# Attention and MLP in one fused kernel: one table for the order of all engines, banks and places

## The chip, the cores and the metric

The kernel runs on one core of a Trainium2 chip. The core has five engines, each with its own instruction stream that it works through in order: TensorE (PE in the profile) for matmuls, VectorE (DVE), ScalarE (ACT), GpSimd (POOL) and SyncE (SP). Here SP does nothing but issue DMA transfers. ScalarE and GpSimd can issue DMAs too. Engines wait for each other with semaphores. PSUM, into which TensorE writes, is used as a ring of 8 banks of 128 x 512 numbers. The metric is the device time of one execution in microseconds (us).

## The reference, cut to what matters

The shapes are: x 1 x 2048 x 448, wqkv 448 x 1344, wo 448 x 448, w1 448 x 1792, w2 1792 x 448, all in bfloat16; 16 heads of 28 columns.

```python
xn = layernorm(x)
q, k, v = split(xn @ wqkv)                    # 16 heads, Dh = 28
p = softmax(q @ k.T * Dh ** -0.5)             # 2048 x 2048 for each head
s = concat_heads(p @ v) @ wo
g = silu(gelu(xn @ w1 + b1) @ w2 + b2)
out = x + s * g
```

## The kernel before

**Tiling.** The 2048 rows of x are four chunks of 512 rows, the 16 heads are four groups of four. A block is one head group for one chunk of queries, so there are 16 blocks, head group outside, chunk inside. A block has 64 scores; a score is one 128 x 512 tile (128 keys, 512 queries, one head) in one PSUM bank, so the kernel has 1024 of them. ScalarE takes the exponential of 776 scores, two or three banks in one instruction. VectorE handles the other 248, in 62 groups of four, another way: it scales and shifts the score into a 16-bit integer whose bits are those of an approximate bfloat16 exponential. Two further copies of each such group, with a constant added to the bits, stand beside it, and p·v sums all three with differently scaled values. These are the 124 shifted copies. A copy is one VectorE instruction (`fs` with `tensor_scalar` on 128 x 2048 16-bit numbers) or two GpSimd halves (`tensor_tensor` on 128 x 512 32-bit numbers). For 5 groups the two shifted copies are first added to each other, so that p·v has two terms: twice by VectorE, three times by a GpSimd DMA that accumulates. A block's p·v is gathered in a PSUM bank and taken out (evacuated) by VectorE, in one or more parts.

**Last quarter of K.** D = 448 is three slices of 128 rows and one of 64. The 64-row slice of a projection can be done as two matmuls of 32 rows, which stand beside scores in TensorE's row mode, or as one full matmul ("joined" or not in the code; the first are called products in score phases here). A padded score takes q from `qpad` with the other heads' rows at zero and runs in the other mode. Before, 21 scores are of this kind. Seven groups of matmuls of the identity with zeros (`filler`) keep TensorE busy; they compute nothing that is used.

**Order.** `schedule` (L1141) lets generators (`p_score`, `p_expq`, `p_ln`, ...) run against a cost model and so records the operations in `K.ops`; each has an engine, a function, a semaphore count and what it needs. `arrange` (L441) takes each engine's operations in recorded order and reorders them by `ORD` (L15): each number says which of those left comes next. `ORD` has rows for PE, ACT, DVE and POOL and none for SP, so SP issues its DMAs as recorded. `place` (L469) puts uses of PSUM into banks, some by `BANKS` (L89). `emit_all` (L553) then writes the five streams, with a wait for each need not yet covered. Nearly every instruction goes through the small wrapper `_Eng`, which is why the profile shows L258 for all of them.

**Start.** `loads` (L1378) issues the first DMAs. In what follows R*n* is the operation recorded with number *n*. SP issues, in this order:

| loads on SP | what | KB |
|---|---|---|
| R16, R17 | x chunk 0, tiles 0 and 1 | 112 each |
| R21, R22 | first head group's columns of the q and k weights, K slices 2 and 3, into `stg` (named `h` in the profile) | 56, 28 |
| R24 | x chunk 1, tiles 1 to 3 | 336 |
| R25, R26 | v weights | 336, 56 |
| R27, R28 | x chunks 2 and 3 | 448 each |
| R29 to R32 | the other head groups' q and k weights | 3 x 168, 84 |
| R33, R34 | w1 | 1344, 224 |
| R249, R250 | x of chunks 0 and 1, copied from DRAM to the output in DRAM | 448 each |

ScalarE's queue issues R18 (x chunk 0, tiles 2 and 3, 224 KB), R19 and R20 (K slices 0 and 1 of the first head group's weights, 56 KB each) and R23 (x chunk 1, tile 0, 112 KB).

R19 to R22 count on one semaphore, `s_w["wqk"]`, and their reader waits until all four are in:

```python
        lw(0, 4 * DH, K.s_w["wqk"], K.b_stg, 6.1, (ACT, ACT, SP, SP))
```

Readers of `stg` are the ScalarE copies into `wq` and `wk` (128 x 224 twice, 128 x 448 once), after which TensorE can do the first q and k projections, and GpSimd's square of the weights (`h<-h`, 128 x 448), from which come the corrections for q. On ScalarE's stream every exponential stands behind these copies. On GpSimd's stream the selector `bsel`, the fill of `vaug` and the layer norm of part of chunk 1 stand behind the square.

**End.** The last chunk's output goes out in 8 stores of 112 KB, seven on SP and one on ScalarE's queue. Each waits for its own sum on VectorE.

Of the kernel before, what the change touches and what calls it, by code (L numbers as in the profile page):

```python
# [6 lines left out]
dt = mybir.dt  # L7
# [7 lines left out]
ORD = {  # L15
# [39 lines left out]
    ),  # L55
    'ACT': (
# [8 lines left out]
    ),  # L65
    'DVE': (
# [21 lines left out]
TO = ()  # L88
# [10 lines left out]
H = 16  # L99
# [198 lines left out]
class _Kernel:  # L298
# [58 lines left out]
    def add(self, t, need, name):  # L357
# [5 lines left out]
        o.no = name  # L363
        return o

    def to(self, ms, us, at, engines, n, ports):


        K = self
# [2663 lines left out]
```

## Time and profile before

| what | us |
|---|---|
| median of 3 runs (lowest, highest) | 410.63 (409.8, 410.68) |
| span of the profiled execution | 408.0 |
| TensorE busy | 395.1 |
| ScalarE busy | 398.1 |
| VectorE busy | 343.5 |
| GpSimd busy | 194.8 |

The span goes from the first to the last instruction; the time of a run is 2.6 us longer than it (410.63 - 408.0). In the views a row has the line, engine, operation, the program's names of output and input tiles, shapes, and "x" with a count; after the bar come busy us, the mean ns of one, and idle time before them with what ended it. Consecutive ScalarE instructions overlap in the records: the next starts before the last one's end is shown. So its pace is read from start to start. Rows of a timeline begin with the start and the length; rows with a count join instructions that follow each other. Rows of the DMA view have the KB of one transfer and the median time from its issue to its landing.

### The profile page before, as it was taken

To read this page: it belongs to the slowest core of one execution; us is meant where nothing else is said; L and a number is where in the kernel's file an instruction comes from. 1 tells how busy PE (TensorE), PEld (TensorE's weight loads), DVE (VectorE), ACT (ScalarE), POOL (GpSimd) and SP (SyncE) were. 2 spreads that over 40 slices of the span, in tenths; PEclk is the share of its full clock that TensorE was granted. 3 is DMA by queue.
4 is the path that set the end of the run, shared out by engine and by line. 5 is a ranking of instruction groups with operands and counts; after the bars stand their busy time and mean duration, and the time that the engine had idled before them with its cause. 6 is when DMAs were issued, how large, how long until landed. Compare 5 with 4: busy or idle time off the path is not lost.

```text
span 408.0 us, 14601 instructions
## 1 busy us (share of the span) xinstructions
PE 395.1 (97%) x6157; PEld 144.6 (35%) x6157; DVE 343.5 (84%) x596; ACT 398.1 (98%) x409; POOL 194.8 (48%) x221
## 2 busy tenths in 40 slices
PE   6899999999999999999999999999999999999996
PEld 5443233333332333332223444332333323333363
DVE  8967688896679889989898127999998999798976
ACT  5999999999999999999999999999999999999995
POOL 7595457649982563254652231156156013555041
PEclk9999999999999999999999999999999999999999
DMA  8902110000101010100331100220010003200065
GB/s 244 305 2 42 4 31 2 16 20 19 29 3 31 2 25 11 34 2 2 77 116 30 30 3 6 55 53 15 18 34 2 4 31 57 64 20 21 14 114 134
DMA packets 18783, 17.54 MB, mean 43 GB/s; under 512 B 8941, under 2 KB 15421, under 8 KB 18686
## 3 DMA queue, kind: packets, MB, share of 16 engines
q1 hardware_dynamic: 16734, 13.55, 12.0%
q0 software_dynamic: 1008, 2.49, 3.8%
q8 instruction: 48, 0.79, 0.9%
q10 hardware_dynamic: 976, 0.57, 0.5%
q14 instruction: 17, 0.14, 0.1%
HBM read 12.54 MB, written 2.88 MB: 38 GB/s over the span
## 4 chain that ended last, share of the span: by engine, by line
PE 59%; ACT 28%; issue 7%; DVE 4%; DMA 1%; POOL 0%; ACTq 0%; DVEq 0%; POOLq 0%
PE ring L258 59%; ACT P L258 16%; ACT h L258 8%; ACT xnT L258 3%; DVE st L258 1%; DVE h L258 1%; DVE xnT L258 1%; DMA x_sb<-in_A_x_dram 1%; DVE vaug L258 0%; DVE x_sb L258 0%; ACT w L258 0%; DVE qT L258 0%; POOL h L258 0%; DVE mv L258 0%; DVE w L258 0%
## 5 line engine op out<-in xcount | busy, mean ns | idle before, releaser
L258 ACT ACTIVATE P<-ring 128x1024 bf16<-128x1024 f32 (+1 forms) x236 | 253.8, 1246 | 1.0 <-PE ring L258 1.0
L258 PE MATMUL ring<-qT,kT 32*128 32x512 bf16 (+2 forms) x1131 | 131.7, 359 | 4.2 <-ACT P L258 1.0
L258 ACT ACTIVATE h<-ring 128x1024 bf16<-128x1024 f32 (+2 forms) x93 | 101.3, 1204 | 2.0 <-PE ring L258 2.0
L258 PEld LDWEIGHTS ring<-qT,kT 32*128 32x128 bf16 x1131 | 36.3, 91 | 121.8 <-ACT P L258 48.1
L258 DVE TENSOR_SCALAR vaug<-ring 128x512 uint16<-128x512 f32 x92 | 60.8, 683 | 5.5 <-PE ring L258 4.8
L258 PE MATMUL ring<-xnT,w 128*32 128x512 bf16 (+1 forms) x880 | 65.3, 381 | 0.0
L258 PE MATMUL ring<-w,h 128*32 128x448 bf16 x896 | 58.5, 356 | 0.0
L258 PE MATMUL ring<-P,vaug 128*32 128x512 bf16 (+2 forms) x606 | 57.9, 351 | 0.2
L258 POOL TENSOR_TENSOR qT<-x_sb,E_sb 128x512 bf16<-128x512 f32 x15 | 17.4, 1162 | 64.6 <-DMA x_sb<-recs 38.0
L258 ACT ACTIVATE xnT<-ring 128x1024 bf16<-128x1024 f32 (+2 forms) x41 | 47.6, 1199 | 0.5 <-PE ring L258 0.5
L258 POOL TENSOR_TENSOR rc<-rs,mone 128x16 f32<-128x16 bf16 x11 | 33.3, 3023 | 28.7 <-DMA rs<-E_sb 14.6
L258 DVE TENSOR_SCALAR w<-ring 128x512 uint16<-128x512 f32 x52 | 34.5, 683 | 2.0 <-PE ring L258 1.7
L258 PEld LDWEIGHTS ring<-xnT,w 128*32 128x32 bf16 (+1 forms) x880 | 21.7, 96 | 28.0 <-issue 6.6
L258 PEld LDWEIGHTS ring<-w,h 128*32 128x32 bf16 x896 | 19.3, 95 | 24.4 <-issue 14.8
L258 PE MATMUL ring<-h,vaug 128*32 128x512 bf16 x201 | 25.1, 383 | 0.0
L258 PE MATMUL ring<-xnT,wq 128*32 128x512 bf16 (+2 forms) x240 | 22.6, 379 | 0.2 <-DVE w L258 0.2
L258 PEld LDWEIGHTS ring<-P,vaug 128*32 128x32 bf16 x606 | 17.3, 95 | 13.6 <-issue 7.4
L258 PE MATMUL ring<-xnT,wk 128*32 128x512 bf16 (+2 forms) x244 | 21.8, 379 | 0.3 <-DVE xnT L258 0.2
L258 DVE TENSOR_SCALAR h<-ring 128x512 uint16<-128x512 f32 x28 | 18.9, 685 | 3.3 <-PE ring L258 3.0
L258 POOL TENSOR_TENSOR qsq<-qT 128x512 bf16<-128x512 bf16 x12 | 13.0, 1079 | 17.0 <-DVE x_sb L258 13.9
L258 DVE CAST qT<-ring 128x512 bf16<-128x512 f32 x15 | 10.3, 688 | 12.7 <-PE ring L258 12.7
L258 DVE CAST h<-ring 128x512 bf16<-128x512 f32 x24 | 16.5, 688 | 4.8 <-PE ring L258 4.8
(207 smaller groups left out, 616.8 us busy)
## 6 DMA issues: line engine op xcount, KB each, us to landing
x_sb<-recs SPq DMA_DIRECT2D x60, 64.0 KB, 2.1
w<-in_B_w_dram SPq DMA_DIRECT2D x1, 1568.0 KB, 7.3
w<-in_B_w_dram SPq DMA_DIRECT2D x1, 1344.0 KB, 8.7
x_sb<-in_A_x_dram SPq DMA_DIRECT2D x2, 448.0 KB, 6.6
out_dram<-in_A_x_dram SPq DMA_DIRECT2D x2, 448.0 KB, 10.6
out_dram<-h POOLq DMA_DIRECT2D x4, 224.0 KB, 4.6
out_dram<-h SPq DMA_DIRECT2D x7, 112.0 KB, 4.4
xnT<-wq POOLq DMA_DIRECT2D x1, 512.0 KB, 6.6
```

Source lines behind the costliest of these rows:

```text
L258: return lambda *a, **k: f(*[real(x) for x in a], **{n: real(x) for n, x in k.items()})
```

## The change

`ORD`, `TO` and `BANKS` go. One table, `PLAN`, takes their place. It is one list of some 3,000 tokens, and the streams of all five engines, SP included, are filled by walking along it. `R`*n* keeps the recorded operation *n* (with its banks behind a slash); the other letters build operations anew: `S` a score, `C` a padded score, `X` exponentials on ScalarE with the cells they are written to, `A` a VectorE score, `H` a shifted copy on VectorE, `G` one half of a shifted copy on GpSimd, `M` the addition of two shifted copies on VectorE, `V` a p·v product, `E` an evacuation of a block, `P`, `J` and `Q` a projection's full matmul, its 32-row halves, and its evacuation. The list begins:

```diff
-ORD = {
...
-TO = ()
-BANKS = {
...
+PLAN = """
+    R0 R16 R24 R2 R28 R5 R4 R6 R3 R18 R1 R35/6 R19 R20 R23 R36/6 R37/6 R250 R17 R29 R39/6 R262 R7 R38 R42 R8 R27 R21 R30 R294 R33 R31 R32 R9 R34 R10
+    R11 R25 R26 R22 R40/6 R41/6 R15 R46 R44/6 R45/6 R50 R48 R47/6 R43 R49/6 R53 R51/6 R52 R54/6 R81 R57/6 R60 R55 R58 R56 R59/6 R64 R61/6 R99 R68/6
...
```

The new `arrange` walks along the table and appends each operation to its engine's stream; for a kept operation it takes the needs over, for a new one it works them out from what last used the bank, the cell or the copy's place:

```diff
-            for d in ORD.get(name, ()):
-                at.append(left.pop(d))
...
+        plan = [(x[0], *([int(z) for z in y.split(",") if z] for y in x[1:].split("/"))) for x in PLAN.split()]
...
+        for x in plan:
...
+                ps = range(4) if t == "H" else range(4 // PH * a[2], 4 // PH * a[2] + 4 // PH)
...
+                o = new(DVE if t == "H" else POOL, fn, need, ("h", m0), True)
...
+            seq[o.E].append(o)
+        K.emit_all(seq)
```

`emit_all` now puts one wait per semaphore ahead of an instruction, that for the highest count, where before it put one for each need not yet covered.

The work changes in these counts:

| | before | after |
|---|---|---|
| exponential instructions of ScalarE: two banks, three, one | 286, 68, 0 | 275, 67, 25 |
| scores handled by VectorE | 248 | 248 |
| shifted copies by VectorE, by GpSimd | 92, 32 | 53, 71 |
| additions of two copies: VectorE, GpSimd DMA | 2, 3 | 6, 0 |
| projections whose last slice stands in score phases | 14 | 11 |
| padded scores | 21 | 12 |
| filler groups | 7 | 0 |
| evacuations of blocks by VectorE | 34 | 29 |

SP's first DMAs now come in this order (R294 is a load of b1 in 1792 pieces of two bytes, 3.5 KB, which before was issued 40 us into the run): R16, R24, R28, R250, R17, R29, R27, R21, R30, R294, R33, R31, R32, R34, R25, R26, R22. R249 comes near the end of the kernel. ScalarE's queue still issues R18, R19, R20, R23, now ahead of its table load. On GpSimd's stream the square of the weights (R81) is followed by R82, R12, R13, R83, R14 (`bsel`), R84, then the fills of `vaug` and the layer norm (R120, R132, R124, R136).

SP's last stores come in the order R3054, R3075, R3031, R3037, R3025, R3062, R3094, where before it was R3025, R3031, R3037, R3054, R3062, R3075, R3094. The VectorE sum ahead of R3075 (R3074) is third from last on VectorE. One multiplication of silu (R3071, 128 x 448 on ScalarE), which before came after the last exponential, now stands between the exponentials near the end.

More of the change, by code (lines that the diff above doesn't have):

```diff
@@ L98 @@
+"""
 D = 448
@@ L239, in get @@
     def get(self):
-        i = self.use.base + self.off if self.off is not None else slice(self.use.base, self.use.base + self.use.n)
+        p = self.use.pos
+        i = p[self.off] if self.off is not None else slice(p[0], p[-1] + 1, p[1] - p[0] if len(p) > 1 else 1)
         x = self.ring[:, i, :]
@@ L277 @@
 class _Op:
-    __slots__ = ("E", "fn", "sem", "by", "cnt", "need", "dur", "lat", "mode", "rows", "port", "start", "kind", "fixed", "spec", "banks", "use", "no", "turn")
+    __slots__ = ("E", "fn", "sem", "by", "cnt", "need", "dur", "lat", "mode", "rows", "port", "start", "kind", "fixed", "spec", "banks", "use", "no", "turn", "rd", "wr")
 class _Task:
@@ L336, in op @@
         o.sem, o.cnt = h if h else (None, 0)
+        if spec and spec[0] in ("exp", "a", "h", "evac", "last"):
+            for b in writes:
+                self.first_w.setdefault(id(b), ([b.w] if b.w is not None else []) + [x for x in b.r if x is not None])
         o.need = [("X", x) for x in self.pre[E]]
@@ L441, in arrange @@
-    def arrange(self):
-        seq = {}
-        for x in TO:
-            (self.to if len(x) > 2 else self.join)(*x)
-        self.chain_up()
-        for E, name in ((PE, "PE"), (ACT, "ACT"), (DVE, "DVE"), (POOL, "POOL"), (SP, "SP")):
-            lst = [o for o in self.ops if o.E == E]
-            at, left = [], list(range(len(lst)))
-            for d in ORD.get(name, ()):
-                at.append(left.pop(d))
-            seq[E] = [lst[i] for i in at + left]
-        self.place(seq)
-        self.emit_all(seq)
@@ L542, in chain_up @@
-    def chain_up(self):
-        chain = [o for o in self.ops if o.port and o.start is not None]
-        for at, o in sorted(self.put_port[::-1], key=lambda x: -x[0]):
-            chain.insert(at, o)
-        last = {}
-        for o in chain:
-            for E, kind in ((POOL if o.E == DVE else DVE, "P"), (o.E, "Q")):
-                if E in last:
-                    o.need.append((kind, (last[E].sem, last[E].cnt)))
-            last[o.E] = o
+        of = lambda h: K.by_h[(id(h[0]), h[1])]
@@ new lines, in arrange, with kind @@
+        K.number()
+        name = lambda o: o.fn.__qualname__.split(".<locals>.")[0].split(".")[-1] + ("" if o.fn.__qualname__.endswith("<lambda>") else "." + o.fn.__qualname__.split(".")[-1])
+        evac = {o.spec[1]: o for o in K.ops if o.spec and o.spec[0] == "ev" and not (o.spec[1][0] == "qk" and o.spec[1][2] == 0)}
+        keys = sorted(evac, key=str)
+        core = ("s", "sc", "exp", "a", "h", "evac", "last")
+        def kind(o):
+            s = o.spec
+            if name(o) == "filler.f" or o.kind == "x" or name(o) == "p_expq" and s is None:
+                return "gone"
+            if not s:
+                return "rest"
+            if s[0] == "pv":
+                return "rest" if s[2][0][0] // 64 == NBLK - 1 else "core"
+            if s[0] in core:
+                return "core"
+            if s[0] in ("pr", "ev") and s[1] in evac:
+                return s[0]
+            return "rest"
@@ new lines, in arrange @@
+        kd = {id(o): kind(o) for o in K.ops}
+        writer, unit_at, opens = {}, {}, {}
+        for o in K.ops:
+            if o.spec and o.spec[0] in ("s", "sc", "pv"):
+                for b, (_, h) in zip(o.rd, [x for x in o.need if x[0] == "R"]):
+                    if kd[id(of(h))] in ("rest", "ev"):
+                        writer.setdefault(id(b), {})[(id(h[0]), h[1])] = h
+            if o.spec and o.spec[0] == "h":
+                unit_at.setdefault(o.spec[1], {}).update({o.spec[5]: o.spec[2], o.spec[4]: 0})
@@ new lines, in arrange @@
+        final = {o.spec[1]: o for o in K.ops if o.spec and o.spec[0] == "last"}
+        plan = [(x[0], *([int(z) for z in y.split(",") if z] for y in x[1:].split("/"))) for x in PLAN.split()]
+        ops, seq = {o.no: o for o in K.ops}, {E: [] for E in (PE, ACT, DVE, POOL, SP)}
+        full = {x[1][0] for x in plan if x[0] == "P" and x[1][1] == KT - 1}
+        merged = {x[1][0] for x in plan if x[0] == "M"}
+        grouped = {x[1][0] // 4 * 4 for x in plan if x[0] == "A"}
+        left = [sum(1 for x in plan if x[0] == "V" and x[1][0] // 64 == b) for b in range(NBLK)]
@@ new lines, in through @@
+        def through(p):
+            c, s = kd[id(p)], p.spec
+            if c == "rest" or c == "ev":
+                return [p]
+            if c == "pr":
+                return [evac[s[1]]]
+            if c == "core" and s[0] == "last":
+                return [p]
+            if c == "core" and s[0] in ("s", "sc", "pv"):
+                b = (s[1] if s[0] != "pv" else s[2][0])[0] // 64
+                return [final[b]] if b in final else []
+            return []
+        was = {id(o): list(o.need) for o in K.ops}
@@ new lines, in arrange @@
+        K.ops = [o for o in K.ops if kd[id(o)] == "rest" or o in list(evac.values()) or o in list(final.values())]
+        bank = {i: [] for i in range(NRING)}
+        cell, lane = {}, {}
+        sc, ex, ap, sh, pads, acc, burst, begun, part = {}, {}, {}, {}, {}, {}, {}, {}, set()
+        pr, done, last_pad, port, e1 = {}, set(), [], None, None
+        pad_of = [o for o in K.ops if name(o) == "p_pad" and o.E == SP]
+        shc = [o for o in K.ops if name(o) == "p_pad.f"][0]
+        vs = {o.spec[1:]: o for o in K.ops if o.spec and o.spec[0] == "vs"}
@@ new lines, in new, with take, cells @@
+        def new(E, fn, need, spec, port=False):
+            K.n_new += 1
+            o = K.op(E, fn, (K.evsem[E], 10 ** 6 + K.n_new), 1, (), (), "t", 0.1, 0.05, "", (), port, spec=spec)
+            o.need += need
+            return o
+        def take(i):
+            need = [("A" if p.E != PE else "W", H(p)) for p in bank[i]]
+            bank[i] = []
+            return need
+        def cells(cs):
+            reg, k = K.pslots[cs[0]]
+            n = len(cs)
+            st = cs[1] - cs[0] if n > 1 else 1
+            return reg[:, k:k + st * (n - 1) + 1:st, :]
@@ new lines, in used, with room @@
+        def used(x):
+            return [("A", H(p)) for p in [p for p in x if not p.spec or p.spec[0] not in ("exp", "a")] or x]
+        def room(toks, at, key):
+            if key in at:
+                return used(at[key])
+            need, seen = [], set()
+            for b in toks:
+                for h in first.get(id(b), ()):
+                    for p in through(of(h)):
+                        if id(p) not in seen:
+                            seen.add(id(p))
+                            need.append(("A", H(p)))
+            return need
@@ new lines, in lanes, with begin @@
+        def lanes(u):
+            if 11 <= u <= 13:
+                return [NP + 42 - F0 + 4 * (u - 11) + k for k in range(4)]
+            if 14 <= u <= 15:
+                return [NP + 56 - F0 + 4 * (u - 14) + k for k in range(4)]
+            return []
+        def begin(u):
+            cs = lanes(u)
+            need = []
+            if cs:
+                for c in cs:
+                    need += room([K.b_P[c]], cell, c)
+            else:
+                need += room(K.b_U[u], lane, u)
+            for c in cs:
+                cell[c] = []
+            lane[u] = []
+            return need
@@ new lines, in touch, with score @@
+        def touch(u, o):
+            lane[u].append(o)
+            for c in lanes(u):
+                cell[c].append(o)
+        first = K.first_w
+        def score(m, b, pad):
+            b0, j, pc, _, _ = K.pieces(m)
+            g, c = b0 // C, b0 % C
+            tk = K.t_score([m], {m: K.ring[:, b, :]}, [], 1)
+            need = take(b)
+            if pad:
+                (t, _, _, _), = pc
+                fn = lambda eng: _mm(eng, K.ring[:, b, :], K.kT[:, g, 128 * t:128 * t + 128], K.qpad[:, :], True, True)
+                need.append(("R", H(pad_of[b0 - 2])))
+            else:
+                fn = tk.fn
+            for tok in tk.reads:
+                need += [("R", h) for h in writer[id(tok)].values()]
+            o = new(PE, fn, need, ("s", (m,)))
+            if pad:
+                pads.setdefault(b0, []).append(o)
+            bank[b] = [o]
+            sc[m] = (o, b)
+            return o
@@ new lines, in sums, with f, fall @@
+        def sums(b, es, acc):
+            fl = []
+            for kk in range(4):
+                for m, v, f0, src in es:
+                    _, j, pc, _, s = K.pieces(m)
+                    g = b // C
+                    if kk >= len(pc):
+                        continue
+                    t, q0, nq, col = pc[kk]
+                    w = K.vs[:, g % 2, K.vt[g].index(t), j, :] if v else K.vaug[:, t, 4 * g + j, :]
+                    def f(eng, j=j, q0=q0, nq=nq, col=col, src=src, w=w, t=t, f0=f0[kk]):
+                        return eng.matmul(acc[32 * j:32 * j + 32, q0:q0 + nq], w, src[:, col:col + nq] if len(src.shape) == 2 else
+                                          src[:, col // 128:(col + nq) // 128, :], tile_position=(0, 32 * j), start=f0, stop=(t == T - 1),
+                                          skip_group_check=True)
+                    fl.append(f)
+            def fall(eng):
+                ins = None
+                for f in fl:
+                    ins = f(eng)
+                return ins
+            return fall
@@ L569, in emit_all @@
                         done[id(p.sem)] = p.cnt
-                        self.prog[E].append(lambda eng, s=p.sem, c=p.cnt: eng.wait_ge(s, c))
+                        most[id(p.sem)] = p
+                for p in most.values():
+                    self.prog[E].append(lambda eng, s=p.sem, c=p.cnt: eng.wait_ge(s, c))
                 if o.sem is None:
@@ L1567, in proj @@
         full = K.t_proj(which, g, c, bank, tok, 3, prio)
-        es, a = K.rest(tok, mm, full.reads, prio, full.fn)
+        es, a = K.rest(tok, mm, full.reads, prio, full.fn, full.spec)
         for k in (1, 2):
@@ L1807, in boot, with rest @@
         return self.b_qT[0][1].tw is not None
-    def rest(self, tok, mm, reads, prio, full):
+    def rest(self, tok, mm, reads, prio, full, spec):
         K = self
@@ L1837, in finish @@
             yield ("until", lambda: K.apart(tok))
-            yield _Task(PE, e["f"], reads, [tok], 0.218, 0.17, prio, mode="row", rows=[e["row"]])
+            yield _Task(PE, e["f"], reads, [tok], 0.218, 0.17, prio, mode="row", rows=[e["row"]], spec=e["spec"])
         return True
@@ L1857, in p_q @@
         qr = _Buf()
-        yield _Task(DVE, lambda eng: eng.tensor_copy(qb, bank), [tok], [qr], 0.7, 0.0, dp)
+        yield _Task(DVE, lambda eng: eng.tensor_copy(qb, bank), [tok], [qr], 0.7, 0.0, dp, spec=("ev", ("qk", 0, g, c)))
         K.banks.append((bank, tok))
@@ L1949, in p_v1 @@
         tk = _Task(PE, K.t_v([t], 4, 16, bank, tok, range(3)), rd, [tok], 0.435, 0.17, K.held("v", t))
-        tk.parts = [(K.t_v([t], 4, 16, bank, tok, (kt,)), rd, [tok], 0.145, (), None, ()) for kt in range(3)]
+        tk.parts = [(K.t_v([t], 4, 16, bank, tok, (kt,)), rd, [tok], 0.145, (), ("pr", ("v", t), kt), ()) for kt in range(3)]
         yield tk
@@ L1971, in p_f1 @@
         full = K.t_f1(c, ft, bank, tok, 3)
-        es, a = K.rest(tok, mm, full.reads, K.held("f1", c, ft), full.fn)
+        es, a = K.rest(tok, mm, full.reads, K.held("f1", c, ft), full.fn, full.spec)
         for k in (1, 2):
@@ L2169, in fall @@
             return ins
-        return _Task(PE, fall, rd, tok_of, 0.218 + 0.001 * len(fl), 0.17, prio, mode="row", rows=[p[2] for p in ps])
+        return _Task(PE, fall, rd, tok_of, 0.218 + 0.001 * len(fl), 0.17, prio, mode="row", rows=[p[2] for p in ps], spec=("s", tuple(ms)))
     def p_scores(self):
```

676 lines of the change are left out of this document (488 added, 188 removed), and 71 rows, old and new, of tables (BANKS, ORD).

## The prediction

> **What bounds the kernel now.** First the page's totals and its chain of waits.
>
> ```profile
> PE 395.1 (97%) x6157; PEld 144.6 (35%) x6157; DVE 343.5 (84%) x596; ACT 398.1 (98%) x409; POOL 194.8 (48%) x221
> ...
> PE 59%; ACT 28%; issue 7%; DVE 4%; DMA 1%; POOL 0%; ACTq 0%; DVEq 0%; POOLq 0%
> ```
>
> TensorE and ScalarE are both full, and the chain changes between them. To see what a better order could give, I take the span in three stretches: up to the first exponential, up to the end of the exponentials, and the end. These are the windows of the second and third stretch (length, then PE, weight loads, DVE, ACT, POOL, TensorE clock, DMA share, GB/s).
>
> ```profile
> 12.58:401.73 389.15, 383.58 (x5987) 136.53 (x5983) 329.43 (x548) 388.43 (x385) 183.85 (x190) 1.00 0.15 35
> 401.73:408.00 6.27, 2.71 (x68) 1.51 (x68) 3.33 (x8) 1.72 (x4) 1.04 (x1) 0.90 0.34 109
> ```
>
> ScalarE's busy time holds overlaps, so I read its pace from starts (timeline of ScalarE), and its work from the groups by shape.
>
> ```profile
> 398.59 1.06 ACT L258 ACTIVATE xnT<-ring 128x1024 bf16<-128x1024 f32 x1
> 399.49 2.41 ACT L258 ACTIVATE P<-ring 128x1024 bf16<-128x1024 f32 x2
> 401.73 0.63 ACT L258 ACTIVATE w<-w 128x448 bf16<-128x448 bf16 x1
> ```
>
> ```profile
> L258 ACT ACTIVATE P<-ring 128x1024 bf16<-128x1024 f32 x190 | 194.0, 1156 | 1.0 <-PE ring L258 1.0
> L258 ACT ACTIVATE h<-ring 128x1024 bf16<-128x1024 f32 x76 | 80.3, 1149 | 0.0
> L258 ACT ACTIVATE P<-ring 128x1536 bf16<-128x1536 f32 x46 | 74.4, 1618 | 0.0
> L258 ACT ACTIVATE xnT<-ring 128x1024 bf16<-128x1024 f32 x32 | 35.4, 1146 | 0.0
> L258 ACT ACTIVATE h<-ring 128x1536 bf16<-128x1536 f32 x15 | 23.6, 1573 | 0.0
> L258 ACT ACTIVATE h<-h 128x1536 bf16<-128x1536 bf16 x8 | 11.9, 1486 | 0.0
> L258 ACT ACTIVATE xnT<-ring 128x1536 bf16<-128x1536 f32 x7 | 11.3, 1614 | 0.0
> L258 ACT ACTIVATE w<-w 128x1792 bf16<-128x1792 bf16 x3 | 5.5, 1848 | 0.0
> L258 ACT ACTIVATE h<-h 128x1024 bf16<-128x1024 bf16 x4 | 4.4, 1096 | 0.0
> L258 ACT ACTIVATE w<-w 128x1344 bf16<-128x1344 bf16 x1 | 1.5, 1500 | 0.0
> L258 ACT ACT_TABLE_LOAD x1 | 1.3, 1283 | 0.0
> L258 ACT ACTIVATE h<-ring 128x448 bf16<-128x448 f32 x2 | 1.1, 544 | 2.0 <-PE ring L258 2.0
> ```
>
> A two-bank exponential costs 0.90 us (398.59 to 399.49); the next two, one of two banks and one of three, take 2.24 to 401.73, so three banks cost 1.34. The stretch of 389.15 then holds 298 two-bank instructions x 0.904 = 269.4 and 68 three-bank ones x 1.33 = 90.4; gelu and silu of stored values, 12 + 4 instructions, some 22 (11.9 + 4.4 + 5.5 + 1.5, less overlap); two table loads 2.6. That is about 384.5: **ScalarE is idle for some 5 us in 389**. Nothing in the change takes work from ScalarE, so a perfect order gains 5 us there, 1.2%. VectorE and GpSimd have room (84% and 48%); what they save reaches the time through these 5 us alone. The rest of the time is the start (12.58) and the end (6.27).
>
> **The change part by part.**
>
> *The middle.* ScalarE: 11 two-bank instructions and one of three go, 25 of one bank come. A one-bank one isn't in the trace; from three to two banks the step falls by 0.43, so 0.47 to 0.48 for one bank; the upper end is a busy 0.54, that of the 128x448 evacuation in the end. 25 x 0.48 - 11 x 0.904 - 1.34 = **+0.7 us** (by 0.54, +2.2).
>
> ```profile
> L258 DVE TENSOR_SCALAR h<-w 128x2048 uint16<-128x2048 uint16 x8 | 5.4, 683 | 0.0
> L258 DVE TENSOR_SCALAR x_sb<-vaug 128x2048 uint16<-128x2048 uint16 x16 | 12.4, 779 | 0.1
> L258 DVE TENSOR_TENSOR x_sb<-x_sb 128x2048 bf16<-128x2048 bf16 x1 | 1.2, 1212 | 0.0
> L258 POOL TENSOR_TENSOR x_sb<-w,shc 128x512 int32<-128x512 int32 x12 | 12.2, 1040 | 6.5 <-PE ring L258 2.7 <-DVE x_sb L258 1.6 <-DVE w L258 1.4
> L258 DVE COPY wv<-ring 128x512 f32<-128x512 f32 x12 | 8.2, 683 | 0.7 <-PE ring L258 0.6
> ```
>
> VectorE loses 39 copies (0.68 to 0.78, together 28) and five evacuations (3.4) and gains four additions (4.8): 343.5 falls to 317. GpSimd gains 78 halves x 1.04 = 81 and comes to about 275, still under 70% of the span. TensorE loses the fillers; nine padded scores and three pairs of 32-row products become other matmuls of like length, so I take nothing. All this lies beside ScalarE's work. It may shorten ScalarE's waits: between 0 and 5 us gained, less what copies made late cost p·v. I take 1, leaving **4 idle**.
>
> Here a rule of the Trainium skill speaks against the change. The row: copies from `vaug` last 779 ns, others 683, so some 0.1 us is lost when two engines meet. The Trainium skill, "SBUF — State Buffer", section "SBUF: two separate sides", says that VectorE's fast copies and GpSimd share a port pair as an exclusive lock, whose loser blocks for the whole instruction. As a mechanism here it is the third rival below.
>
> *The start.* SP now issues the last of the four loads that open the first head group's weights (R22, 28 KB) as its 17th instead of its 4th DMA. These are the rows of SP's timeline, its DMA view to 25 us, and the one of b1's load at 40 us.
>
> ```profile
> 2.12 0.75 SPq L258 DMA_DIRECT2D h<-in_A_wqkv_dram  x1
> 8.14 1.46 SPq L258 DMA_DIRECT2D w<-in_B_w_dram  x2
> 9.64 1.23 SPq L258 DMA_DIRECT2D out_dram<-in_A_x_dram  x2
> ```
>
> ```profile
> w<-in_B_w_dram SPq DMA_DIRECT2D x1, 1344.0 KB, 8.7
> w<-in_B_w_dram SPq DMA_DIRECT2D x1, 224.0 KB, 10.2
> h<-in_A_wqkv_dram SPq DMA_DIRECT2D x1, 84.0 KB, 7.0
> h<-in_A_wqkv_dram SPq DMA_DIRECT2D x1, 56.0 KB, 2.9
> h<-in_A_wqkv_dram SPq DMA_DIRECT2D x1, 28.0 KB, 4.0
> ```
>
> ```profile
> b1h<-in_B_b_dram SPq DMA_DIRECT2D x1, 3.5 KB, 4.4
> ```
>
> ```profile
> 0.00:3.00 3.00, 0.00 (x0) 0.00 (x0) 1.88 (x12) 1.28 (x1) 1.91 (x11) 1.00 0.33 87
> 3.00:12.00 9.00, 8.35 (x98) 6.33 (x98) 8.28 (x30) 6.44 (x20) 7.64 (x20) 1.00 1.04 314
> 12.00:21.00 9.00, 7.94 (x166) 3.81 (x166) 9.00 (x26) 8.64 (x12) 4.40 (x8) 1.00 0.81 279
> ```
>
> R22 was issued at 2.12 and had landed 4.0 later. A load issued behind others waits for their bytes: 84 KB took 7.0, 224 KB behind 1344 took 10.2, and the DMA engines were full (share 1.04) from 3 to 12 us at 314 GB/s, then 279. Now 4,540 KB stand on SP up to and with R22, and 448 KB on ScalarE's queue beside them, in all 4,990 KB or 5.1 MB. By 12 us about 3.1 MB are in (9 us x 314, and 3 us x 87); the other 2.0 MB take 6.4 to 7.2 us: 18.4 to 19.2. R294, 1792 tiny pieces that took 4.4 alone for 3.5 KB, also stands ahead; I add 1 for it (0 to 2.5). **R22 lands at about 20** instead of 6.1. The lower bound is SP's own issuing: 16 issues ahead at some 0.6 each (1.46 / 2, 1.23 / 2) put its issue at 10 to 11, and 2.9, the 56 KB's landing, gives 13.
>
> What stands behind it are ScalarE's copies of these weights, and through them every projection and score.
>
> ```profile
> 7.05 0.37 ACT L258 ACTIVATE wq<-h 128x224 bf16<-128x224 bf16 x1
> ...
> 12.58 2.85 ACT L258 ACTIVATE P<-ring 128x1024 bf16<-128x1024 f32 x3 [0.36 <-PE ring L258]
> ```
>
> From the first copy to the first exponential it took 5.53. In the changed kernel the layer norm of chunk 0 is done by then, but the square, `bsel` and the corrections for q on GpSimd and VectorE start late too; I take 5.0. **First exponential at 25 instead of 12.58: 12.4 us lost.** Nothing hides it: ScalarE has nothing else to do before the scores, and the 384.5 us follow. Chunk 1's layer norm, queued behind the square on GpSimd, may be late for the second set of keys by about 1; that is in the 4 of idle time.
>
> TensorE has nothing to do from about 8 to 20. In the window of the end its granted clock is 0.90, so it falls when idle. The first projections and scores, some 4 us of work, would run slower; I add **1** (0 to 2). The Trainium skill, "TensorE: Matmul & The Clock Gate", section "What's actually happening", states half clock after an idle window of about 3.4 us and full clock after as long a busy one; by that it would be an estimated 1 to 2 us.
>
> *The end.* The sums and stores of the last chunk:
>
> ```profile
> 397.21 8.58 SPq L258 DMA_DIRECT2D out_dram<-h  x7
> 405.04 0.39 DVE L258 TENSOR_TENSOR h<-h 128x448 bf16<-128x448 bf16 x1
> ```
>
> Before, six stores were issued before the last sum was ready. Now R3075 waits for R3074, third from last on VectorE (about 404.5 in the old times), and R3031, R3037, R3025 and R3062, long ready, stand behind it, then R3094. Five issues of some 0.4 put the last at 406.9, where it was 405.4: **+1.6** (0 to 2.5). The silu piece at 401.73 moves ahead into an idle gap: nothing.
>
> *Sum.* 25.0 (first exponential) + 1 (clock) + 384.5 + 0.7 + 4 (idle) + 6.3 + 1.6 (end) = 423.1 of span; with the 2.6 outside it **425.5**, +3.6%. The profiled execution (408.0 + 2.6) is the median, 410.6, so no other correction.
>
> **The rivals.**
>
> 1. *The order of the loads is harmless.* R22 needs only 28 KB. If the rings of the DMA engines let a small load pass large ones, or SP's queue weren't kept full, it would land a few us after its issue, or SP's order isn't what the table says. For it: in the trace the 56 KB behind it landed in 2.9. Against: 84 KB in 7.0, 224 KB in 10.2, each where its place in the queue puts it. If R22 lands before about 8, the change decides in the middle: 410.6, less 0 to 5 for a better order, +0.7, +0 to 2.5 in the end: 406 to 414, **around 410 and not slower**, where 3 are gained. The turning point is R22's landing at some 8 to 9 us: each us later adds one.
> 2. *Only SP's issuing counts.* R22 lands at 13, first exponential at 18, TensorE idle for less long: 425.5 - 7 - 1 = **417.5**.
> 3. *The middle gets worse.* If VectorE's 53 copies each wait for a GpSimd half (1.04), 55 us come to its 317, 372 of some 400; it would hold scores back, as GpSimd's copies, two halves 2.08 against 0.7, would hold p·v. I price this at 1.5% of the middle: 425.5 + 6 = **431**. For it: 779 against 683 ns. Against: that excess is 0.1 and not 1.04, and VectorE has 27 us more room than before.
>
> **How the numbers follow.** Late weights, as in the sum: 0.66. Rival 1: 0.13. Rival 2: 0.09. Rival 3: 0.12. The likeliest gives 425.5; its own terms (landing 18.4 to 22, idle 1 to 6, clock 0 to 2, end 0 to 2.5) give 420 to 430. The range 413 to 431 takes in rival 2 and part of rival 3, and leaves out rival 1 and the far side of rival 3, 0.2 together. A measurement of this kernel tells 0.2%, about 0.8 us, from no change. Rival 1 is faster by more in half of its cases and the same in a third: faster 0.07, same 0.04, slower 0.89.
>
> **What would show it.** The first exponential's start near 25 us, ended by a wait that goes back to the load of the weights; R22 issued near 10 and landed near 20. ScalarE's first copy of `wq` just behind. Between first and last exponential 388 to 391 us: more says rival 3 (VectorE's copies above 0.8 us, its busy time above 340), 385 says that the order was worth all of the 5 us. SP's last store issued 5.5 us behind the last exponential's end (before, 405.8 against 401.9: 3.9). Wrong would be a first exponential before 14 us.

## The result, and the profile after

The changed kernel takes 430.37 us (median of 4 runs, 429.38 to 432.4) against 410.57 for the kernel before (median of 4): ratio 1.0496, 95% interval 1.0465 to 1.0527. The forecast was 425.5 with a range of 413 to 431. Direction and range hold; the loss is 19.8 us where 15 were forecast.

These are the totals and the chain of the page after.

```profile
span 427.7 us, 13831 instructions
...
PE 398.9 (93%) x6048; PEld 145.4 (34%) x6048; DVE 328.8 (77%) x554; ACT 398.9 (93%) x422; POOL 270.0 (63%) x296
...
ACT 60%; PE 27%; DVE 4%; DMA 3%; SPq 3%; issue 1%; POOL 0%; DVEq 0%
```

ScalarE has the same busy time as before (398.9 and 398.1) in a span 19.7 longer: all of the loss is idle time of ScalarE. DMA and SP's queue, 1% together before, now have 6% of the chain. The windows of the second and third stretch, cut at the first exponential's start and the last one's end as in the prediction, say where:

```profile
26.04:420.17 394.13, 385.73 (x5896) 136.50 (x5894) 314.82 (x506) 390.10 (x398) 261.05 (x267) 1.00 0.10 25
420.17:427.70 7.53, 2.30 (x68) 1.28 (x57) 3.16 (x7) 1.09 (x2) 0.00 (x0) 0.94 0.38 123
```

| stretch | before | after | difference |
|---|---|---|---|
| to the first exponential | 12.58 | 26.04 | +13.5 |
| first to last exponential | 389.3 | 394.1 | +4.8 |
| the end | 6.1 | 7.5 | +1.4 |

(The prediction's window of the second stretch ended at 401.73; the last exponential's record ends at 401.90, which is used here for both.)

The start, on ScalarE's timeline and SP's:

```profile
11.71 0.20 ACT L384 ACTIVATE rstd<-lnv 128x2 f32<-128x2 f32 x1
19.63 0.39 ACT L384 ACTIVATE wq<-h 128x224 bf16<-128x224 bf16 x1 [7.71 <-DMA h<-in_A_wqkv_dram]
...
26.04 4.79 ACT L384 ACTIVATE P<-ring 128x1024 bf16<-128x1024 f32 x6 [0.50 <-PE ring L384]
```

```profile
5.67 0.63 SPq L384 DMA_DIRECT2D b1h<-in_B_b_dram  x1
6.34 3.86 SPq L384 DMA_DIRECT2D w<-in_B_w_dram  x1
...
13.38 0.62 SPq L384 DMA_DIRECT2D h<-in_A_wqkv_dram  x1
```

The load of the weights (R22) was issued at 13.38 and landed at 19.6, and the copy that waits for it started 0.03 later: its idle time of 7.71 is ended by that load. The issue of the 1344 KB of w1 alone held SP for 3.86, where before the two loads of w1 took 1.46 together. The bytes ahead don't explain that: 2,300 KB stood ahead of w1 on SP here and 2,520 KB before. What stands right ahead of it here is R294, the load of b1 in 1792 pieces. In every profile with R294 there (e2, e3, e8 and e9 below too) the issue took 3.83 to 4.36. In e1, where R294 comes behind, both loads of w1 took 1.24:

```profile
8.48 1.24 SPq L384 DMA_DIRECT2D w<-in_B_w_dram  x2
```

No run moves R294 alone. The windows from 9.5 to 11.5 us, after and before, show its pieces on the DMA engines (the last two columns are their busy share and GB/s):

```profile
9.50:11.50 2.00, 0.29 (x3) 0.30 (x4) 1.53 (x7) 1.65 (x7) 0.00 (x0) 0.70 1.01 98
9.50:11.50 2.00, 2.00 (x33) 1.49 (x35) 1.90 (x10) 1.92 (x6) 1.88 (x5) 1.00 1.11 368
```

The engines are full in both, but move 98 instead of 368 GB/s (e1, whose R294 comes later, moves 347 there): an estimated 1.5 us of transfer time for the pieces (2.0 x (1 - 98 / 368)).

The middle has one long stall between exponentials that the kernel before doesn't have, at 35 to 42 us. ScalarE's timeline, then VectorE's and GpSimd's:

```profile
31.64 4.70 ACT L384 ACTIVATE P<-ring 128x1024 bf16<-128x1024 f32 x5
38.34 1.08 ACT L384 ACTIVATE P<-ring 128x512 bf16<-128x512 f32 x2 [2.00 <-PE ring L384]
39.89 1.02 ACT L384 ACTIVATE P<-ring 128x1024 bf16<-128x1024 f32 x1 [0.46 <-PE ring L384]
41.61 3.90 ACT L384 ACTIVATE P<-ring 128x1024 bf16<-128x1024 f32 x6 [0.70 <-PE ring L384]
```

```profile
32.96 0.39 DVE L384 TENSOR_SCALAR h<-x_sb,mv,rstd 128x448 bf16<-128x448 bf16 x1
...
34.47 2.61 DVE L384 TENSOR_SCALAR h<-x_sb,mv,rstd 128x448 bf16<-128x448 bf16 x1
```

```profile
34.52 2.42 POOL L384 TENSOR_TENSOR h<-h 128x1344 bf16<-128x1344 bf16 x1
```

And TensorE's:

```profile
37.13 0.63 PE L384 MATMUL ring<-ident,h 128*128 128x128 bf16 x8 [1.88 <-DVE h L384]
```

A normalisation of the same shape takes VectorE 0.39 and, 1.5 us later, 2.61. The second ends just behind GpSimd's square of the other head groups' weights (R218). TensorE's transposes wait for it, the scores stand behind them, and ScalarE waits 2.00, 0.46 and 0.70. From the starts (steps of 0.904 for two banks, 0.478 for one) this costs ScalarE 2.2 + 0.6 + 0.8 = 3.6 us.

### The profile page after: what moved, and what is told of

Same layout as the page of the kernel before. It is cut to its first block, busy times and chain, and to the rows that moved or that the text cites. A ratio compares the mean times of both kernels' runs of the same rounds, so it can differ in the third digit from the quotient of the medians.

```text
span 427.7 us, 13831 instructions
## 1 busy us (share of the span) xinstructions
PE 398.9 (93%) x6048; PEld 145.4 (34%) x6048; DVE 328.8 (77%) x554; ACT 398.9 (93%) x422; POOL 270.0 (63%) x296
## 4 chain that ended last, share of the span: by engine, by line
ACT 60%; PE 27%; DVE 4%; DMA 3%; SPq 3%; issue 1%; POOL 0%; DVEq 0%
ACT P L384 47%; PE ring L384 27%; ACT h L384 10%; SPq L384 3%; ACT xnT L384 2%; DMA h<-in_A_wqkv_dram 1%; DVE h L384 1%; DMA x_sb<-recs 1%; DMA recs<-rc 1%; ACT w L384 1%; DVE st L384 1%; DVE kT L384 0%; DVE w L384 0%; DVE qsq L384 0%; POOL qT L384 0%
## 5 line engine op out<-in xcount | busy, mean ns | idle before, releaser
L384 ACT ACTIVATE P<-ring 128x1024 bf16<-128x1024 f32 (+2 forms) x308 | 298.1, 1148 | 4.5 <-PE ring L384 4.4
L384 PE MATMUL ring<-P,vaug 128*32 128x512 bf16 (+2 forms) x746 | 66.7, 352 | 0.4 <-DVE x_sb L384 0.4
L384 ACT ACTIVATE h<-ring 128x1024 bf16<-128x1024 f32 (+3 forms) x55 | 62.9, 1218 | 2.1 <-PE ring L384 2.1
L384 PE MATMUL ring<-xnT,w 128*32 128x512 bf16 x888 | 64.1, 381 | 0.1
L384 DVE TENSOR_SCALAR x_sb<-ring 128x512 uint16<-128x512 f32 (+1 forms) x71 | 48.0, 693 | 6.4 <-PE ring L384 5.2
L384 DVE TENSOR_SCALAR h<-ring 128x512 uint16<-128x512 f32 x48 | 32.2, 687 | 7.0 <-PE ring L384 6.2
L384 DVE TENSOR_SCALAR kT<-ring 128x512 uint16<-128x512 f32 (+1 forms) x39 | 26.4, 699 | 6.0 <-PE ring L384 5.9
L384 PEld LDWEIGHTS ring<-xnT,w 128*32 128x32 bf16 x888 | 21.2, 96 | 26.6 <-issue 7.2
L384 DVE TENSOR_SCALAR w<-ring 128x512 uint16<-128x512 f32 x36 | 24.4, 687 | 5.7 <-PE ring L384 5.2
L384 ACT ACTIVATE xnT<-ring 128x1536 bf16<-128x1536 f32 (+2 forms) x20 | 24.3, 1246 | 0.6 <-PE ring L384 0.6
```

What stands on the lines that cost most here:

```text
L384: return lambda *a, **k: f(*[real(x) for x in a], **{n: real(x) for n, x in k.items()})
```

## The experiments

All times below are medians; the kernel before, run beside each group on the same chip, took 410.11 (e1 to e4), 410.43 (e5 to e8) and 410.37 (e9 to e12), so differences across groups are known to some 0.3 us. The edits reorder tokens of `PLAN` unless said otherwise; a diff shows the tokens that change places. "Step" is the time from one ScalarE start to the next, and its excess what it has over 0.904, 0.478 or 1.33 for two, one or three banks.

**e1_loads: SP's first loads as before.** R249 stays near the end, and R294 comes behind R250. SP's tokens, in order:

```diff
-R16 R24 R28 R250 R17 R29 R27 R21 R30 R294 R33 R31 R32 R34 R25 R26 R22
+R16 R17 R21 R22 R24 R25 R26 R27 R28 R29 R30 R31 R32 R33 R34 R250 R294
```

> The changed kernel with SP's first 17 DMAs in the order of before. Theory (the first head group's weights come late): R22 lands near 6 us, the first exponential starts at 12.5 to 14 instead of 26.0, and the time falls by 12 to 17 us, to 413 to 418; the stall of ScalarE at 35 to 41 us, some 3.6 us, may go with it or stay. Rival (the loss sits in the middle, where GpSimd's copies hold others back): the start is shorter, but idle time turns up behind it, and the time stays above 420.

Measured: 417.49 us, with runs of 412.82 (the profiled one) and of 417.3 to 418.8. R22 landed at 6.15 and the first exponential started at 13.38. In the profiled run the stall is absent: ScalarE's excess at that place is 0.05. VectorE's and GpSimd's timelines show why:

```profile
21.92 0.38 DVE L384 TENSOR_SCALAR h<-x_sb,mv,rstd 128x448 bf16<-128x448 bf16 x1
```

```profile
22.07 2.52 POOL L384 TENSOR_TENSOR h<-h 128x1344 bf16<-128x1344 bf16 x1
```

Here VectorE came 0.15 ahead of GpSimd and took 0.38, and GpSimd took 0.10 more than in the changed kernel. By the medians the loads are worth 12.9, within the 12 to 17 that were expected, and the kernel has a race of two engines. The three other runs are 4.5 to 5.9 us above the profiled one. That is more than a stall of 3.6; they have no trace, so how much of it is the race isn't shown.

**e2_w_only: the weights alone early.** R21 and R22 behind R16, the rest as changed.

```diff
-R16 R24 R28 R250 R17 R29 R27 R21 R30 R294 R33 R31 R32 R34 R25 R26 R22
+R16 R21 R22 R24 R28 R250 R17 R29 R27 R30 R294 R33 R31 R32 R34 R25 R26
```

> The changed kernel with R21 and R22 alone put second and third on SP; all else of SP's order as changed. Theory: the weights land at about 5 us, and the next late thing is x chunk 0 tile 1 (R17), which landed at 8.4 in the changed kernel and now lands near 9: the first layer norm is 4 us later than before, the first exponential starts at 16 to 18, and the time is 419 to 423. Rival (the weights alone set the start): first exponential at 12.5 to 14, 414 to 418.

Measured (one run): 425.07; the weights had landed by 5.9, and yet the first exponential started at 22.11. Both theories missed. VectorE's timeline, then TensorE's:

```profile
10.00 0.63 DVE L384 BATCH_NORM_STATS2 st<-x_sb 128x6 f32<-128x448 bf16 x1 [5.85 <-DMA x_sb<-in_A_x_dram]
```

```profile
17.86 0.28 PE L384 MATMUL ring<-qsq,bsel 128*128 128x256 bf16 x1
21.14 0.58 PE L384 MATMUL ring<-wv,xnT 128*32 128x112 bf16 x32 [3.00 <-DMA wv<-in_A_wqkv_dram]
21.65 0.39 PE L384 MATMUL ring<-qT,kT 32*128 32x512 bf16 x3
```

The theory was right about x: its tile 1 (R17) landed at 9.98, where e1 has 4.09, and the first `wq` copy, behind the layer norm on ScalarE, started at 13.44 instead of 8.36. That is 5.1 of the 8.7 us by which this start is later than e1's. It left out v: the first v projection stands ahead of the first scores on TensorE, and its weights (R25, R26), here the last two on SP, cost another 3.0. So late loads hid behind each other: in the changed kernel R17 landed at 8.36, v's weights at 19.42 and R22 at 19.6. To mend the one moved the first exponential by 3.9 us, to mend the whole order by 12.7 (e1).

**e3_before_loads: the kernel before with the changed order of loads.** A row for SP in `ORD`:

```diff
+    'SP': (0, 3, 6, 13, 0, 5, 4, 0, 3, 25, 5, 3, 3, 3, 1, 1, 0, 0,),
```

> The kernel of before with SP's first 18 DMAs in the order of the changed kernel and nothing else. Theory: the first exponential starts at 25.5 to 27, and the time is 423 to 427, 13 to 16 us over the kernel before: the order of the loads alone carries two thirds or more of the loss. Rival (the start costs what it does only with the changed orders on the other engines): under 420.

Measured: 424.43, ratio 1.034 (1.0311 to 1.0368); R22 landed at 20.15, the first exponential started at 27.27. **The order of the loads alone costs 14.3 us**, with nothing else of the change. The start is 0.3 later than the theory's 25.5 to 27, the time is within its 423 to 427.

**e4_loads_stores: e1, and the last stores as before.**

```diff
-R3054 R3075 R3031 R3037 R3025 R3062 R3094
+R3025 R3031 R3037 R3054 R3062 R3075 R3094
```

> As the first of these runs, and SP's seven last stores in the order of before too. Theory: 1 to 1.6 us below the first of these runs, from a last store that is issued some 4 us behind the last exponential's end instead of 5.5. Rival (the stores hide behind each other and behind ScalarE's store): no difference beyond 0.5 us.

Measured: 416.27, 1.2 below e1, but the race above is in both, so the medians don't settle it. The traces do: from the last exponential's end to the end of the span 7.6 in e1 (403.3 to 410.9) and 6.2 in e4 (407.5 to 413.7), as expected 1.4. The profiled run of e4 fell on the other side of the race:

```profile
21.95 2.61 DVE L384 TENSOR_SCALAR h<-x_sb,mv,rstd 128x448 bf16<-128x448 bf16 x1
```

```profile
22.01 2.42 POOL L384 TENSOR_TENSOR h<-h 128x1344 bf16<-128x1344 bf16 x1
```

VectorE's record starts 0.06 ahead, not 0.15, and it has the 2.61 of the changed kernel; ScalarE's excess there is 2.0 + 0.6 + 1.0.

**e5_square: e4, and R218 at another place.**

```diff
-R180 R170 R173 R184 R189 R218
+R218 R180 R170 R173 R184 R189
```

> As the fourth run (loads and stores in the order of before), and GpSimd's square of the other groups' weights (R218, 128 x 1344) moved ahead of the layer norm of chunk 2, into a gap in which GpSimd waits. Theory (a VectorE normalisation that starts just behind this GpSimd instruction is held until it ends, 2.61 us instead of 0.38, and ScalarE then waits 2.0 + 0.6 + 1.0): no normalisation longer than 0.8 us, no idle time of ScalarE over 0.5 us before 30 us, 411 to 413 in every round, the runs closer together. Rival (the gap of ScalarE comes from chunk 2's layer norm being late anyway): the gap stays, 415 to 417.

Measured: 411.94 (12 runs, 411.3 to 412.19), ratio 1.0032 (1.0023 to 1.0042). The runs are within 0.9 us of each other, where e4's were 2.4 and e1's 5.9 apart, and the stall is gone. Two other normalisations took 1.00 and 1.10, which the theory had excluded; no step of ScalarE beside them has an excess over 0.35. The excess of ScalarE from the first exponential to the last is 5.2, less than the 5.9 of the kernel before.

**e6_end: e5, and the end as before.** The silu piece (R3071) goes behind the last exponential, and three operations that stand near its result to their old places.

```diff
-R3071 X1009,1010/0,17
+X1023/12 R3071
-R3086 R2987
+R3084/3 R3086
-R3025 R3074
+R3069/1 R3074
-R3014 R3080
+R2987 R3080
```

> As e5, and the end of the kernel in the order of before: the silu piece R3071 behind the last exponential, R3074 and R3086 where VectorE had them, R3080 last on GpSimd. Theory (the silu piece takes 0.7 us of ScalarE's time between the exponentials, and behind them it stood in idle time): 0.5 to 1.4 below e5. Rival (TensorE sets the pace there, since ScalarE waits 0.8 us for it right behind the piece): within 0.4 of e5.

Measured: 413.2, 1.3 **above** e5, a miss of both. ScalarE has one step with 1.79 of excess at 394.7, where the silu piece had stood. TensorE and GpSimd there:

```profile
395.97 0.37 PE L384 MATMUL ring<-wo,qT 128*32 128x448 bf16 x4 [1.02 <-POOL qT L384]
```

```profile
394.77 1.15 POOL L384 TENSOR_TENSOR qT<-x_sb,E_sb 128x512 bf16<-128x512 f32 x1 [8.33 <-DMA x_sb<-recs]
```

The product for the output waits for reciprocals that come by DMA. On SP the last of their four loads stands behind the last load of x (R2984, 448 KB), where before it stood ahead of it.

**e10_recs: e6, and that load behind the reciprocals.**

```diff
-R2984 R2942
+R2942 R2984
```

> As e6, and on SP the last load of x (R2984, 448 KB) behind the last of the four loads of reciprocals (R2942) instead of ahead of it. Theory (that load delays the last reciprocals, GpSimd's product of q waits for them, TensorE for that: ScalarE's 1.8 us of idle time at 395 us in e6, where the silu piece stood before): the gap falls by 0.7 to 1.8 us and the time with it, 411.4 to 412.5. Rival (the gap comes from something else that is late): no change from e6, 413.

Measured: 411.57, 1.6 below e6 (1.2 by the ratios to the kernel before, 1.0062 and 1.0033); the gap falls from 1.79 to 0.59. So the silu piece in the changed kernel stood in a gap that another edit of the same table had made.

**e7_copies: e5, with 39 copies back on VectorE.** 78 `G` tokens become 39 `H` tokens at the place of the second half, for instance:

```diff
-G60,1,0/5 ... G60,1,1/5
+H60,1/5
```

> As e5, but 39 of the 71 shifted copies of GpSimd are made by VectorE again (each at the place of its second half), so 92 and 32 as in the kernel before. Theory (both engines are off the path, ScalarE's idle time is some 5 us with either division): within 1.5 us of e5, VectorE busy near 355, GpSimd near 190. Rival 1 (GpSimd's copies hold p.v back): 2 us or more below e5. Rival 2 (VectorE's room is what the change lives on): 2 us or more above e5.

Measured: 427.72, 15.8 above e5, which is rival 2. VectorE is busy for 351.4, 83%, so it isn't full; but its stream is in order, and ScalarE's excess comes in some twenty places (20.8 us in all, where e5 has 5.2). One of them, on TensorE and on VectorE:

```profile
284.59 0.39 PE L384 MATMUL ring<-qT,kT 32*128 32x512 bf16 x3 [1.48 <-DVE x_sb L384]
```

```profile
281.69 1.55 DVE L384 TENSOR_SCALAR x_sb<-xnT 128x2048 uint16<-128x2048 uint16 x1
283.17 0.78 DVE L384 TENSOR_SCALAR kT<-wq 128x2048 uint16<-128x2048 uint16 x1
283.87 0.67 DVE L384 TENSOR_SCALAR x_sb<-ring 128x512 uint16<-128x512 f32 x1
```

A VectorE score (the last row) holds a PSUM bank until it is done, and here it stands behind two copies. By this place, what GpSimd's copies buy in this plan is that VectorE empties banks in time. The old plan did that with 92 copies on VectorE, in its own order; the run doesn't say what 92 copies would cost in a plan made for them.

**e8_after_square: the changed kernel with R218 alone moved**, as in e5's diff.

> The changed kernel with R218 alone moved as in e5; the loads stay late. Theory: the stall at 35 to 41 us goes, 3 to 4 us below the changed kernel, 426 to 428. Rival (with late loads chunk 2's layer norm is late anyway): 429 to 431.

Measured: 427.77, 2.6 below the changed kernel, where 3 to 4 were expected: the stall is gone (no excess over 0.4 before the last exponential), though the first exponential started 0.7 later (26.71) in the profiled run.

**e9_warm: e8, with TensorE kept busy.** In `arrange`, for the last warm-up matmul ahead of the weights; the matmul runs 55 times, and the 54 more compute nothing that is used:

```diff
                 o = ops[a[0]]
+                if a[0] == 134:
+                    o.fn = lambda eng, f=o.fn: [f(eng) for _ in range(55)][-1]
```

> As e8 (late loads, R218 moved), and 55 matmuls of the identity where the last of the warm-up matmuls ahead of the weights stands, so that TensorE is busy while it waits for R22; nothing uses them. Theory (the halved clock of 12 to 24 us costs some 1 us, as the sum had it): granted clock 1.00 from 17 to 26 us, 5.2 to 6 us from R22's landing to the first exponential where it was 6.4 in the changed kernel, the time 0.7 to 1.5 below e8. Rival (the chain runs through the other engines): clock 1.00, but less than 0.4 us gained.

Windows of e8 first, then of e9 (the seventh column is the granted clock):

```profile
17.00:21.00 4.00, 0.00 (x0) 0.00 (x0) 0.00 (x0) 0.60 (x2) 0.55 (x1) 0.50 0.59 130
21.00:24.00 3.00, 2.56 (x20) 2.13 (x21) 1.69 (x7) 2.00 (x5) 2.67 (x7) 0.50 0.00 0
```

```profile
17.00:21.00 4.00, 3.47 (x32) 2.85 (x30) 0.00 (x0) 0.09 (x1) 0.05 (x1) 1.00 0.69 149
21.00:24.00 3.00, 1.81 (x22) 1.37 (x22) 1.69 (x7) 2.78 (x7) 2.67 (x7) 1.00 0.02 5
```

From the first `wq` copy to the first exponential e8 took 6.31 (20.40 to 26.71) and e9 5.47 (20.91 to 26.38): the halved clock costs 0.8 in that stretch, as the theory has it. The time is 427.74, no different from e8, as the rival has it: R22 landed at 20.88 instead of 20.38 in the profiled runs, and the rest of the gain doesn't show. For the whole kernel the clock's price stays open, between nothing and 0.8.

The column of the granted clock doesn't tell all of it. These are four matmuls of the k projection in e8, e9 and e3:

```profile
23.23 1.06 PE L384 MATMUL ring<-xnT,wk 128*128 128x256 bf16 x4
22.94 0.60 PE L384 MATMUL ring<-xnT,wk 128*128 128x256 bf16 x4
23.22 1.06 PE L259 MATMUL ring<-xnT,wk 128*128 128x256 bf16 x4
```

e3's windows show a granted clock of 1.00 from 8 to 31 us, and yet its four take 1.06 as in e8, behind 7.76 us without work. Its weights came as late, so what it lost at the start includes the slower matmuls too.

**e11_start_end and e12_start: ScalarE's start as before.** e11 on e10, e12 on e5 with e10's edit:

```diff
-R18 R19 R20 R23 R15 R50 R43 R53
+R15 R18 R19 R20 R23 R43 R50 R53
```

> As e10, and on ScalarE the table load first and the first sum of chunk 0 (R43) ahead of R50, as before. Theory (the first exponential is 0.8 to 1.0 us later than before for this order): first exponential at 12.5 to 12.9, 0.7 to 1.0 below e10. Rival (GpSimd's order sets the start): less than 0.3.

> As e5, with R2984 behind R2942 and the start of ScalarE as in e11, but the end of the kernel as changed (silu piece between the exponentials). Theory: 0.8 to 1.2 below e5, 410.8 to 411.2, no more than 0.2% from the kernel before: what is left of the change is worth nothing, since ScalarE's idle time between the first and the last exponential is some 5 us with both plans. Rival (GpSimd's copies are a gain that the other losses hid): 409.5 or less.

Measured: e11 411.56, no gain over e10 although the first exponential starts at 12.69 instead of 13.57: the 0.9 is given back at the end (7.3 from the last exponential's end to the end of the span, 6.2 in e10), where TensorE waits 0.97 and 0.75 for VectorE; why is not shown. e12 410.6 (11 runs), 1.3 below e5 (1.2 by the ratios), with the first exponential at 12.94; ratio to the kernel before 1.0004 (0.9995 to 1.0013). Its window from the first exponential to the end of the last:

```profile
12.94:402.84 389.90, 384.01 (x5896) 136.62 (x5894) 312.13 (x507) 389.76 (x398) 261.12 (x267) 1.00 0.13 31
```

389.9 us, where the kernel before has 389.3. No version measured here beats the kernel before; e12 equals it.

## Why the prediction was right, and where a term was mis-sized

The mechanism of the start, which carries most of the loss, is shown by e1 and e3. That the range held is partly luck. The time lies 0.6 below the top of the range and just above the 420 to 430 of the sum's own terms. The top was there for rival 3, whose price was worked out for copies that wait, and the copies are not what cost the time. (The terms add up to 423.1, with 2.6 to 425.7 and not 425.5.)

The 19.8 us, by the runs: the loads and stores 15.8 (e8 to e5), R218's place 2.6 (changed kernel to e8), ScalarE's start and the reciprocals 1.3 (e5 to e12), and 0.2 left, which can't be told from nothing. The parts belong to this order of mending. The loads alone in the kernel before cost 14.3 (e3), and the stores 1.4 (e1 and e4), together the 15.8 again.

| term of the sum | forecast | measured |
|---|---|---|
| R22 lands | 20 | 19.6 |
| from there to the first exponential, with the clock | 5 + 1 | 6.4 |
| ScalarE's work and idle time to the last exponential | 384.5 + 0.7 + 4 | 394.1 |
| the end | 6.3 + 1.6 | 7.5 |
| median less the profiled span | 2.6 | 2.7 |

The last row isn't all time outside the span. Each run on record of the kernel before beside the experiments, 46 in all, took 1.75 to 1.96 longer than its own span, and the profiled run of the changed kernel took 429.57, 1.9 more. The rest is the median above the profiled run. So the profiled 408.0 belongs to a run near 409.8, and not to the median as the prediction took it.

- **The start** was right in mechanism and size. R22's issue was taken at 10 to 11 and came at 13.38, since SP itself was held up at w1; the landing went by bytes, as forecast, with an estimated 1.5 for R294's pieces where 1 was added. Rival 1 (the order is harmless) is out by e3, rival 2 (only SP's issuing counts) by the landing 6.2 behind the issue. Not seen: v's weights were as late, and x's tile 1 would have been next (e2). ScalarE's own order costs another 0.9 only where the loads are early (13.57 in e10, 12.69 in e11). In the changed kernel the layer norm of chunk 0 "is done by then", as the prediction has it: its last ScalarE instruction ended at 11.91, and the weights landed at 19.6.
- **The clock** was right in sign; 1 in the sum, 0.8 in the stretch that e9 shows. The Trainium skill, "TensorE: Matmul & The Clock Gate", section "What's actually happening", states half clock after an idle window. The granted clock of 0.50 in e8 behind idle time agrees, and e3's column of 1.00 doesn't, though its matmuls are as slow.
- **The middle** is the step that was mis-sized: "leaving 4 idle" became 8.9 (394.1 - 385.2). The 4.9 more are two places: 3.6 are the stall at R218 (e8 and e5 take it away), and 1.45 is the step of the silu piece, 0.67 of its own and 0.78 of waiting for TensorE: "moves into an idle gap: nothing" was right about the gap, but the gap was a new one (e6, e10).
- **Rival 3** named the right mechanism at the wrong place. A copy of VectorE does seem to wait at times for a GpSimd instruction (one took 1.55 in e7, beside one of 1.04), and VectorE's busy time came to 328.8 where 317 were worked out; but in the changed kernel its copies took 0.74 on average, 4 of 53 over 0.8, and lay beside ScalarE's work. So of the prediction's signs of this rival one came, more than 391 us between first and last exponential, and two didn't. What cost time was one normalisation on the path against one long GpSimd instruction. The Trainium skill, "SBUF — State Buffer", section "SBUF: two separate sides", has this rule: the loser blocks for the whole instruction. Here the trace agrees: 2.61 against 0.38, for a GpSimd instruction of 2.42. The price of 6 was meant for the copies, so that the middle came out 4.9 too long is near it by luck. The chance of 0.12 was too low, because the rule was weighed by the mean of the copies (779 against 683 ns) and not by asking which long GpSimd instruction stands beside work on the path.
- **The end**: 1.6 forecast, 1.4 measured, by e1 and e4 due to the order of the stores. SP's last store was issued 5.6 behind the last exponential's end, where the prediction has 5.5.
- **The rest of the diff**, copies and additions, one-bank exponentials, banks and the order of the middle, comes to nothing that can be measured when taken together: with the side effects undone (e12) the two kernels are equal, and ScalarE's excess is 5.2 where it was 5.9. The runs don't part these pieces, and e7 shows that in this plan the 39 copies can't simply go back to VectorE.

## What to carry to other kernels

When one table orders every queue, read the order of the loads first: here 28 KB landed only behind the 4.5 MB ahead of it, and late loads hid behind each other until all were mended. An engine off the path can be relieved without any gain if another engine works without pause (VectorE from 343.5 to 325.8 us in e12); look at the start-to-start pace of that one before pricing the rest. Keep a long GpSimd instruction away from a short VectorE instruction on the critical path: in these traces about a tenth of a us decided whether the short one took 0.38 or 2.61.

## What was not expected of the hardware

The blocked VectorE instruction is shown long, not late: its record starts 0.05 or 0.06 ahead of GpSimd's (34.47 and 34.52, 21.95 and 22.01) and it still waits, while with 0.15 it goes first (21.92 and 22.07). That fits the runs of e1, 412.8 to 418.8 us, and those of e5, 411.3 to 412.2, though only the profiled ones show which engine went first. A load of 3.5 KB in 1792 pieces is dear: in each of the five profiles in which the load of w1 was issued right behind it, that issue took 3.83 to 4.36 us, and in the changed kernel the full DMA engines moved 98 GB/s for two us. And TensorE ran at half pace in e3 without a sign of it in the granted clock.
